# Twelve rewritten round orders, one rounding moved to ScalarE and one subtraction moved to VectorE in a fused attention and ReGLU kernel

## The chip, the cores and the metric

The kernel runs on one core of one Trainium2 chip. The metric is the device time in microseconds (us) of one execution of the whole program; lower is better. The core has five engines with a queue each: TensorE (PE) multiplies, VectorE (DVE) and ScalarE (ACT) work element by element and can read TensorE's results, GpSimd (POOL) works element by element on the on-chip memory alone and issues DMAs, and SyncE (SP) issues DMAs. Every queue is worked off strictly in the order written.

## The reference

```python
x = A_x                                              # 2048 x 448, float32
g = sigmoid((x * gate_w).sum(-1))
qkv = x @ wqkv                                       # 16 heads of 28
p = softmax(q @ k.T * 28 ** -0.5); a = (p @ v) @ wo  # per head, 2048 x 2048
gate, up = B_x @ W_gate, B_x @ W_up                  # F = 1792; B_x is not used: x stands for it
b = (relu(gate) * up) @ W_down
out = g * a + (1 - g) * b
```

In `reference` the second block is called with the same `x`, so both halves read one input.

## The kernel before, in words

**Precision.** Most products are computed from a rounded high part and the remaining low part of each operand. Making such a pair is always two instructions: `act_high` (or `dve_high`) writes the rounded copy, then `low` (VectorE) or `pool_low` (GpSimd) subtracts it from the source.

**Stages.** (1) Up to 140 us: projections of q, k, v and the gate, written to DRAM, with the first 100 row-maximum matmuls and the first scores mixed in. (2) From 140 to 1051 us: 32 attention rounds, two per head, which also compute 54 of the 56 gate/up tiles. (3) The tail, from 1051 us on: the last two gate/up tiles, the down projection (`down`) and the output projection (`wout`).

**A round.** A round handles 8 of the 16 key tiles of a head. Its work is written by hand in a string, and `ROUNDS` says which string each round uses. Every letter emits one step, and the order of the letters is the order in which every engine's queue is filled:

- `s` + bank: a 128x512 score matmul; ScalarE takes it out with an exponential (`scores`, L265 and L267).
- `m` + bank: a row-maximum matmul for the next head; VectorE reduces it (`smax`, L242 and L243).
- `r` + bank: a score matmul whose softmax shift is not known yet; ScalarE copies it out raw (`raw_scores`, L273 and L277). `d` is VectorE's running maximum over it (`raw_max`, L281), and the bank is free only after both.
- `e`: ScalarE's exponential of a raw tile (`raw_exp`, L304), after GpSimd subtracted the shift from it (`raw_less`, L300).
- `x`: one of the 10 full-height matmuls of a gate or an up half (`gu_mm`, L612). Ten accumulate in one bank. A round with 40 of them holds banks 4, 5, 6 and 7 in turn; a round with 20 holds 4 and 5.
- `u`, `U`, `l` (first round only): the splitting of gate/up weight tiles 0 and 1 (`split_f`) and a delayed store of the projections.

There are eight PSUM banks. The digit behind a letter is its bank; in the listings below, the banks 0 to 7 are called `b_69` to `b_76`. Banks 0 to 3 are always open to `s`, `m` and `r`; 6 and 7 only until the round's second tile needs them. A matmul into a bank waits until the engine that reads the bank's last result is done.

Behind the string, a round issues the last, half-height matmul of each gate/up half (two at a time, in the two halves of the array), then `relu` and `hidden`, the splitting of the next round's weight tiles, the exponentials that are left (`while len(exps) > ROUNDS[r + 1].count("e")`: all but those that the next string names), and 64 matmuls that multiply probabilities with V (`pv`, L650), in groups of four side by side. Nothing else for TensorE is issued during `pv`, so the two evicting engines catch up there.

Strings by name: FIRST and SECOND (rounds 0 and 1), AA (rounds 2, 4, 6, 10, 12, 14, 18, 20, 22), BA (3, 7, 11, 15, 19, 23), BB (5, 13, 21), DA (8, 16), BC (9, 17), CA (24, 26), CB (25, 27), AY, BY, AZ, BZ (28 to 31).

**The tail.** `fetch_o` loads a 512-token block of the attention output into the tile `or`, of which there is one buffer; `split_o` makes its high and low parts (`on`) in two pieces; `wout` multiplies them. `split_d` prepares the next hidden tile (`hh`) and, for the first 14, a tile of W_down (`WD`): ScalarE rounds, VectorE subtracts. `fetch_d` loads their sources over the SP queue, two tiles ahead of the `split_d` that uses them. `fetch_o` for the second block stands on the same SP queue, ahead of the loads for the thirteenth hidden tile.

Of the kernel before, what the change touches and what calls it, by code (L numbers as in the profile page):

```python
# [45 lines left out]

FIRST = ("m2m3m6m7s0s1uxxxxs0xm2lxxxxUs3xxs6s1m7xm0xs2m3xs1m7xxm2xxr0r1r3xm7s2dxr0dxxr7ds2xr1dxr3xs2dxr0dxxxdm"
         "2s1xm3xxm0s1xm2xm3xm1s0xxm2xm3s0xm1xs2m0m2m1m0")  # L50

SECOND = ("xs0r1m2s6xm7dxs3xs0m2r6xs7m3dxs1xm0xs2m7xs3r1m6xs0xds2xm7xs3m6r0s1xxdm2s7xm3s1xr0s7xm2dxs1m3xs7xm2s1"
          "xs0r7m3xs1xdm2s0xm3s1xxm0r2xs1s3dxm0xxs1m2s3xm0xs1r2m3xs0xds1xm3xs0m2s1xxxm0s2")

AA = ("xm0s1xr2m6s7xm3xs1xm2s0xr7m6xs1dxm3s0xm2xr6s1xm7dxs0m3xs2m1xr7exm0s2dxm3s1exxm0s2xr7em1s3xdm2xes0xm1"
      "xs3xexm2r0s1m3xdexs2xm1s3xexm0r2m1s3xdexm0xxs3em1s2xxm0s3xm1s2xm0xxr1s2m0d")
# [4 lines left out]
BA = ("xs0m1r2s7xm6ds3xs0m1r7xs6m3ds0xr2s1m6xds3xm0s7xr1s6m3s2dxm7s0xr6s3m2xds1m0xs7r3xs2m1s6dxm7s0r2xs1m6x"
      "ds3m0xs7r1s6xm2xds7m0xs6")

AY = ("xs0m1s2xr6m7s3m0xs2r6xm1s3s7dxm2r0s1xm3ds7xm6s2r1s3xm7xds0m2s6r3xes7m0xds1m6xem2s0xr7s3s1xm6des0m2xs"
      "3xm6es1xm7em0xs2r3s6xm1r7xds2s0m1m6d")

BY = ("xs0r1ds2xs6xr7ds3xs0xs2r6ds1exs3xs0r7dexs2s1xxr6des3xs0xs7xr2des1xs6xs3xs0xr7ds2s1s6xxr0dxs2s7s1")

AZ = ("xs0xs1xxs2xxs6xs7xxs3xs0xxs1xxs2xs7xxs3xs0xxs1xxs2xs3xxs0xxs1xs2exxs3xs0exxs1xxs2exs0xxs1xx")

BZ = ("xs0xs1xxs2xxs6xs7xxs3xs0xxs1xxs2exs7xxs3xes0xxs1xxes2xs3xxs0exxs1xs2xexs3xs0xxs1xxs2xs0xxs1xx")

DA = ("xs0m1xs2r6m7xxm3s0xm2xs1r6m7xs0xdm3xs2r1m7xs0m6dxxs3m2xs7xm0r3xs1m2dxm7s0xr1xs2xdm0m3xs7m2xs1xem0r7x"
      "s3m1exds2xm0s3r1xexm2xdm3s0exxm2xxs0em1s3xxm2s0exm1r3xs2em0xds1xxm2s0xm1")

BC = ("xm0s1r2xm7s6xdxm3s1xem0xs7r6m2exs1xdm3xs0em7xr2xs6m1xds3m0xxm7s1xr3xm2s0dxm1s7xm2xs0xm3r7xs1m0dxs2xm"
      "3xs1m0xr2xm3s1dxm0xxs3m1xs2xr0m3xs1dm2xxs3xm1s0xm2r3xs1m0dxs2xxs1m0")

CA = ("xm0s1xr2m6s7xm3xs1m2xs0xr7m6xs1dm3xm0s2xxr6m1s7xdm3xs2xm0s7xr1m2xs3dxm7s0xm2xs3r1m0exs7xdm2xs3em0xr1"
      "m7xs2em3xds0xxem2xm3s0m1xexs2xr0m3xes1dm2xxs3xem1s0xm2m3xes1m0xs2xxm1xr0s2m1d")  # L80

CB = ("xs0m1r2s7xm6ds3xm0s1r7xes6m3s2dxm1exr0s3m6xs7s2dxm1exr6m3xs7s0s2dm1xr3xs7m6s0xdm2s1xr7s6m0s3dr1xs2xm"
      "6s0dm3s7xm2s6r0xs7m1xds6xm2s7")
# [17 lines left out]
def gated_mix_kernel(ctx, tc, x, wq, wo, wgu, wd, out):  # L101
# [55 lines left out]
    def low(dst, src, high):  # L157
        nc.vector.tensor_tensor(dst, src, f32(high), op=OP.subtract)  # L158

    def pool_low(dst, src, high):  # L160
        nc.gpsimd.tensor_tensor(dst, src, f32(high), op=OP.subtract)  # L161
# [426 lines left out]
    def split_f(i, high, low, part=(0, 1)):  # L588

        if part[0] == 0:  # L590
            WS[i] = fe.tile([P, 2, 7, P], F32R, name=f"wg_{i}", tag="wg", bufs=2)
        w, wr = WS[i], WR[i]
        for s in part:
            high(w[:, s, 0:3], wr[:, s, 0:3])
            low(w[:, s, 3:6], wr[:, s, 0:3], w[:, s, 0:3])
        if part[-1] == 1:
            high(w[:, :, 6], wr[:, :, 3])
            for s in range(2):
                rows = lane(1 - (2 * i + s in SECOND))
                low(w[rows, s, 6], wr[rows, s, 3], w[rows, s, 6])  # L600
            del WR[i]
# [206 lines left out]
    ON, OR, GA, DR, HH, ACC = {}, {}, {}, {}, {}, {}  # L808
# [191 lines left out]
```

## Time and profile before

| what | value |
|---|---|
| median of 3 runs | 1241.53 us (1241.13 to 1241.87) |
| the profiled execution's own time | 1241.64 us |
| its span, first to last instruction | 1239.9 us |
| granted TensorE clock | 1.00 in every slice |
| busy: PE, PE weight loads | 1228.2 us, 858.5 us |
| busy: DVE, ACT, POOL | 896.9, 842.9, 627.5 us |
| matmuls with weight loads | 6447 |

The times and the profile come from one program without any other load on the chip. A row of the timeline gives the start, the length, the engine, the line, the operation, the tiles (written <- read), the count of instructions that were merged into the row, and in brackets the engine's idle time ahead of it with what ended it. Consecutive matmuls overlap in the records (a 128x512 matmul's record is 0.39 us long, but the next begins about 0.23 us after it), so a small brake on TensorE shows in the distance between starts and hardly in the busy share.

### The profile page before, as it was taken

Reading aid. Unit: us, or ns where it says so; the run is one execution under the profiler, and the core shown is the slowest. Engines: PE = TensorE matmul, PEld = TensorE weight load, DVE = VectorE, ACT = ScalarE, POOL = GpSimd, SP = SyncE. Lnnn points to the kernel's source line nnn. Section 1 sums busy time; section 2 is a strip of 40 time slices with the busy share of each in tenths; the row PEclk is TensorE's granted clock in tenths of the full one; section 3 lists DMA queues with packets and bytes.
Section 4 is the critical chain, followed back from the end, with each engine's and each line's share of the span. In section 5 each row is a group of like instructions: output and inputs, shape, how many; then the busy total and the mean of one; then the engine's idle time right before and its main releaser. Section 6 shows DMA issues by size and latency. Waiting matters only on the chain.

```text
span 1239.9 us, 18801 instructions
## 1 busy us (share of the span) xinstructions
PE 1228.2 (99%) x6447; PEld 858.5 (69%) x6447; DVE 896.9 (72%) x1442; ACT 842.9 (68%) x1673; POOL 627.5 (51%) x702
## 2 busy tenths in 40 slices
PE   9999999999999999999999999999999999999998
PEld 6888766666656665666666666666565655989997
DVE  6488879787878787797878787878787734563342
ACT  5312667988797877968787988797887895522121
POOL 4332325574738384838384665647482677431020
PEclk9999999999999999999999999999999999999999
DMA  8966514141434232333524141425231122853432
GB/s 308 344 240 245 179 52 153 54 129 60 137 95 145 75 122 82 107 97 107 166 96 135 57 129 60 137 80 159 75 110 43 48 85 91 273 172 110 140 107 80
DMA packets 62035, 157.64 MB, mean 127 GB/s; under 512 B 12994, under 2 KB 19746, under 8 KB 57514
## 3 DMA queue, kind: packets, MB, share of 16 engines
q1 hardware_dynamic: 47924, 111.47, 29.0%
q0 software_dynamic: 13584, 44.52, 9.9%
q8 instruction: 50, 0.82, 0.3%
q10 hardware_dynamic: 432, 0.46, 0.1%
q14 instruction: 45, 0.37, 0.1%
HBM read 108.70 MB, written 48.16 MB: 127 GB/s over the span
## 4 chain that ended last, share of the span: by engine, by line
PE 83%; ACT 7%; DMA 3%; POOL 3%; DVE 2%; issue 1%; SPq 0%; DVEq 0%; POOLq 0%; ACTq 0%
PE b L612 17%; PE b L650 16%; PE b L242 13%; PE b L265 12%; PE b L900 9%; PE b L436 6%; PE b L273 4%; ACT P L267 3%; PE b L454 3%; PE b L855 3%; ACT P L304 1%; POOL V L300 1%; ACT V L304 1%; ACT V L277 1%; DVE wg L155 1%
## 5 line engine op out<-in xcount | busy, mean ns | idle before, releaser
L243 DVE TENSOR_REDUCE mx<-b 128x1 f32<-128x512 f32 x784 | 519.2, 686 | 61.9 <-PE b L242 55.4
L267 ACT ACTIVATE P<-b 128x512 f32<-128x512 f32 x780 | 446.7, 610 | 130.1 <-PE b L265 115.3
L612 PE MATMUL b<-X,wg 128*128 128x512 f32 (+1 forms) x1232 | 429.5, 400 | 0.3 <-POOL wg L161 0.3
L242 PE MATMUL b<-K,Q 128*128 128x512 f32 x784 | 310.6, 399 | 2.8 <-DVE mx L243 1.4
L265 PE MATMUL b<-Q,K 128*128 128x512 f32 x784 | 309.9, 398 | 1.1 <-ACT P L267 0.8
L612 PEld LDWEIGHTS b<-X,wg 128*128 128x128 f32 (+1 forms) x1232 | 219.6, 188 | 62.2 <-issue 22.1
L650 PE MATMUL b<-P,v 128*32 128x512 f32 x1800 | 226.2, 594 | 0.0
L242 PEld LDWEIGHTS b<-K,Q 128*128 128x128 f32 x784 | 147.0, 188 | 52.5 <-ACT P L267 16.2
L265 PEld LDWEIGHTS b<-Q,K 128*128 128x128 f32 x784 | 146.9, 188 | 48.1 <-ACT P L267 16.4
L634 POOL DMA_DIRECT2D h_d<-rl x56 | 31.4, 561 | 291.0 <-DVE rl L628 248.5
L300 POOL TENSOR_TENSOR P<-P,V 128x512 f32<-128x512 f32 x120 | 150.9, 1293 | 26.6 <-DMA V<-mr_d 26.6
L650 PEld LDWEIGHTS b<-P,v 128*32 128x32 f32 x1800 | 61.7, 110 | 144.4 <-issue 144.2
L161 POOL TENSOR_TENSOR wg<-wgr,wg 128x384 fp32r<-128x384 f32 x216 | 155.0, 732 | 9.8 <-DVE wg L155 1.2
L300 POOL TENSOR_TENSOR V<-V 128x512 f32<-128x512 f32 x120 | 150.8, 1292 | 11.9 <-DMA V<-mr_d 11.9
L281 DVE TENSOR_TENSOR V<-b,V 128x512 f32<-128x512 f32 x215 | 145.9, 679 | 3.3 <-ACT P L277 1.6
L900 PE MATMUL b<-WD,hh 128*128 128x448 f32 x672 | 138.3, 366 | 2.2 <-DVE hh L158 1.4
L900 PEld LDWEIGHTS b<-WD,hh 128*128 128x128 f32 x672 | 126.1, 188 | 13.2 <-DVE hh L158 2.2
L152 ACT ACTIVATE hh<-hr 128x512 fp32r<-128x512 f32 x56 | 35.3, 631 | 110.5 <-PE b L900 106.8
L650 PE MATMUL b<-V,v 128*32 128x512 f32 x248 | 110.1, 593 | 0.0
L273 PE MATMUL b<-Q,K 128*128 128x512 f32 x240 | 96.2, 402 | 0.0
L158 DVE TENSOR_TENSOR hh<-hr,hh 128x512 fp32r<-128x512 f32 x56 | 46.8, 836 | 62.0 <-ACT hh L152 62.0
L277 ACT ACTIVATE V<-b 128x512 f32<-128x512 f32 x116 | 70.1, 609 | 9.6 <-PE b L273 8.7
(100 smaller groups left out, 1125.5 us busy)
## 6 DMA issues: line engine op xcount, KB each, us to landing
wgr<-wgu SPq DMA_DIRECT2D x55, 512.0 KB
K<-qk_d SPq DMA_DIRECT2D x64, 224.0 KB
Q<-qk_d SPq DMA_DIRECT2D x64, 224.0 KB
h_d<-rl POOLq DMA_DIRECT2D x56, 256.0 KB, 3.3
hr<-h_d SPq DMA_DIRECT2D x56, 256.0 KB
qk_d<-st POOLq DMA_DIRECT2D x21, 512.0 KB, 4.9
X<-x_d SPq DMA_DIRECT2D x24, 256.0 KB
x_d<-X POOLq DMA_DIRECT2D x5, 1024.0 KB, 5.6
```

The source lines that it names most:

```text
L161: nc.gpsimd.tensor_tensor(dst, src, f32(high), op=OP.subtract)
L242: nc.tensor.matmul(ps, Q[h][:, u * P:(u + 1) * P], K[h % 3][:, c * TB:(c + 1) * TB], start=True, stop=True)
L243: nc.vector.tensor_reduce(MX[h][:, 4 * u + c:4 * u + c + 1], ps, axis=AX.X, op=OP.max)
L265: nc.tensor.matmul(ps, K[h % 3][:, kt * P:(kt + 1) * P], Q[h][:, j * TB:(j + 1) * TB], start=True, stop=True)
L267: nc.scalar.activation(prob(i, j), ps, AF.Exp, scale=SCALE)
L273: nc.tensor.matmul(ps, K[h % 3][:, kt * P:(kt + 1) * P], Q[h][:, 3 * TB:], start=True, stop=True)
L277: nc.scalar.activation(own, ps, AF.Copy)
L281: nc.vector.tensor_tensor(run, ps, run if i % NK > 1 else prob(i - 1, 3), op=OP.max)
L300: nc.gpsimd.tensor_tensor(own, own, piece(TOP), op=OP.subtract)
L612: nc.tensor.matmul(ps, WS[i][rows, s, a], xf(i // NF, b)[rows], start=(n == 0), stop=(n == NT - 1))
L650: nc.tensor.matmul(po[32 * j:32 * j + 32], VH[h][:, i % NK], prob(i, j), start=(i == i0), stop=(i == i0 + ni - 1))
L900: nc.tensor.matmul(ACC[i // NF][t][:, :D], HH[i][:, a, t * P:(t + 1) * P], WD[:, f, b], start=(f == 0 and n == 0), stop=(f == NF - 1 and n ...
```

## The change

Twelve of the strings are new; BB gets one `d` moved behind one `x`, and BC is dropped, its two rounds now using BB. Each string still holds the same number of `x`, `s` and `r`. SECOND has 27 `m` instead of 25 and the two CA rounds 28 instead of 29, so their sum is the same. The `e` of CB (3), BC (3) and two of BY's four are gone from the strings, and DA has 8 instead of 7, so more exponentials are issued at the end of the round before (CA, DA) or of the same round (BY).

```diff
-FIRST = ("m2m3m6m7s0s1uxxxxs0xm2lxxxxUs3xxs6s1m7xm0xs2m3xs1m7xxm2xxr0r1r3xm7s2dxr0dxxr7ds2xr1dxr3xs2dxr0dxxxdm"
-         "2s1xm3xxm0s1xm2xm3xm1s0xxm2xm3s0xm1xs2m0m2m1m0")
+FIRST = ("m2m3m6m7s0s1uxxxxs0xm2lxxxs7xs0xUxm3xs1m7s6xm2s3m0m7xxxs2m1xm0s7m6r3m2r1xr7xxr3xxr2dr0dr1ddddxxs7xxx"
+         "s3s2xm7m0xxs1m3xxm2xm1s3m0xxm2xr3m1xxdxm0xm2s1")
...
-ROUNDS = [FIRST, SECOND, AA, BA, AA, BB, AA, BA] + [DA, BC, AA, BA, AA, BB, AA, BA] * 2
+ROUNDS = [FIRST, SECOND, AA, BA, AA, BB, AA, BA] + [DA, BB, AA, BA, AA, BB, AA, BA] * 2
...
             elif o == "U":
-                split_f(1, dve_high, pool_low)
+                split_f(1, act_high, pool_low)
...
         act_high(ON[tb][0][:, c], OR[tb][:, c])
-        pool_low(ON[tb][1][:, c], OR[tb][:, c], ON[tb][0][:, c])
+        low(ON[tb][1][:, c], OR[tb][:, c], ON[tb][0][:, c])
```

(The new file is three lines shorter, so its line numbers are lower by three.)

**VectorE in the first round.** Here `wg` is a split weight tile, `wgr` the weights as loaded, `mx` the row maxima and `pair` the delayed store. Before:

```order
L158 TENSOR_TENSOR pair<-b_74,pair 128x512
L155 CAST wg_1235<-wgr_1195 128x384 x2
L155 CAST wg_1235<-wgr_1195 128x2x128
L243 TENSOR_REDUCE mx_931<-b_76 128x1
L243 TENSOR_REDUCE mx_931<-b_69 128x1
```

Now:

```order
L155 TENSOR_TENSOR pair<-b_74,pair 128x512
L240 TENSOR_REDUCE mx_931<-b_72 128x1
L240 TENSOR_REDUCE mx_931<-b_76 128x1
L240 TENSOR_REDUCE mx_931<-b_71 128x1
L240 TENSOR_REDUCE mx_931<-b_69 128x1
```

The three casts of weight tile 1 have left VectorE's queue; they stand on ScalarE's, behind five exponentials of the round and the copy of `pair`.

**TensorE in the middle of a round AA** (round 4; matmuls 61 to 69 of its 99 ahead of the half-height ones, counted from 0). Before:

```order
L242 MATMUL b_71<-K_128,Q_131 128x512
L273 MATMUL b_69<-Q_130,K_127 128x512
L265 MATMUL b_70<-Q_132,K_129 128x512
L242 MATMUL b_72<-K_128,Q_131 128x512
L612 MATMUL b_75<-X_121,wg_2162 128x512
L612 MATMUL b_75<-X_120,wg_2162 128x512
L265 MATMUL b_71<-Q_132,K_129 128x512
L612 MATMUL b_75<-X_120,wg_2162 128x512
L242 MATMUL b_70<-K_128,Q_131 128x512
```

Now, matmuls 61 to 70:

```order
L262 MATMUL b_70<-Q_132,K_129 128x512
L262 MATMUL b_76<-Q_132,K_129 128x512
L239 MATMUL b_72<-K_128,Q_131 128x512
L609 MATMUL b_75<-X_120,wg_2166 128x512
L262 MATMUL b_71<-Q_132,K_129 128x512
L239 MATMUL b_69<-K_128,Q_131 128x512
L262 MATMUL b_70<-Q_132,K_129 128x512
L609 MATMUL b_75<-X_121,wg_2166 128x512
L262 MATMUL b_72<-Q_132,K_129 128x512
L239 MATMUL b_76<-K_128,Q_131 128x512
```

Bank 7 (`b_76`) still takes scores and maxima here, where the old string had only banks 0 to 3 left for them.

**ScalarE at the border of a CA and a CB round** (rounds 24 and 25; `P` are raw score tiles, `mr` the copied maxima that open round 25). Before:

```order
L152 ACTIVATE wg_8090<-wgr_7936 128x2x128
L304 ACTIVATE P_1043<-P_1043 128x512
L304 ACTIVATE P_1085<-P_1085 128x512
L304 ACTIVATE P_1129<-P_1129 128x512
L304 ACTIVATE P_1163<-P_1163 128x512
L304 ACTIVATE P_1208<-P_1208 128x512
L261 ACTIVATE mr_8143<-b_75 12x128
```

Now:

```order
L149 ACTIVATE wg_8090<-wgr_7936 128x2x128
L301 ACTIVATE P_1043<-P_1043 128x512
L301 ACTIVATE P_1085<-P_1085 128x512
L301 ACTIVATE P_1129<-P_1129 128x512
L301 ACTIVATE P_1163<-P_1163 128x512
L301 ACTIVATE P_1208<-P_1208 128x512
L301 ACTIVATE P_1238<-P_1238 128x512
L301 ACTIVATE P_1276<-P_1276 128x512
L301 ACTIVATE P_1327<-P_1327 128x512
L258 ACTIVATE mr_8146<-b_75 12x128
```

All eight exponentials of the second half now stand ahead of `mr`, during `pv`; three of them stood between the scores of round 25.

More of the change, by code (lines that the diff above doesn't have):

```diff
@@ L43 @@
 AHEAD = 100
-FIRST = ("m2m3m6m7s0s1uxxxxs0xm2lxxxxUs3xxs6s1m7xm0xs2m3xs1m7xxm2xxr0r1r3xm7s2dxr0dxxr7ds2xr1dxr3xs2dxr0dxxxdm"
-         "2s1xm3xxm0s1xm2xm3xm1s0xxm2xm3s0xm1xs2m0m2m1m0")
[L52 to L56, printed above, removed]
@@ L58 @@
-BB = ("xs0r1m2xs7m6dxm3xs0xr2s7xm6dxs1m0xm3xs7xm6r1s2xm0dxs7xm3xr2s0m7xds1xm3xm0s7xr1m2xs3dm7xs0xr2m3xs1dxm"
-      "0xxs3m1xs2xxm0r3s1m2xdxs0xxm1s2xm0s3xm1s2xm0r3xm1s2dxs0xxm1m2xs0")
[L61 to L83, printed above, removed]
-ROUNDS = [FIRST, SECOND, AA, BA, AA, BB, AA, BA] + [DA, BC, AA, BA, AA, BB, AA, BA] * 2
+FIRST = ("m2m3m6m7s0s1uxxxxs0xm2lxxxs7xs0xUxm3xs1m7s6xm2s3m0m7xxxs2m1xm0s7m6r3m2r1xr7xxr3xxr2dr0dr1ddddxxs7xxx"
+         "s3s2xm7m0xxs1m3xxm2xm1s3m0xxm2xr3m1xxdxm0xm2s1")
@@ new lines @@
+SECOND = ("xs1m2s0xm6s7m1xs2m3xr6m7ds1m0r2xs3dxs7xs6xm3xm0s1xm2s6m3xs7m0s2r6m1dxs3r7xm0xdr1xs3m6dxs0xs2xs3m6s0m"
+          "7xm1s2xm3xs0xm2s7m1xs0xxm3xm1m0s2r7s3xxr1xs2xddr0m3xxxs2xs1xs3dxxm0xs1m2xs3s0xm1s2")
+AA = ("xs2m7m0s1m6r3xm2s7xm1s3xm0r6xm2r3dxs1s7s0xxxxdxm2es7s3m6s1xm0r2r7m3dxdxxs6xs0xm1m3ees2xxm6xs1s7m0m3x"
+      "m2xeexxs1s7m3xs2m0s1xs3m7r2m0xxm3xr1xeddxxexm3xs2em0xr1xs3xs2edxm0xxm3s1m2")
+DA = ("xs7m6s1xxs3m0s2m7s1xm6m3s2xr7s0xm6xr2m7dr3s1s6m0xxdr7xm1s2s0xxm6xm2s3s1xs0xdm6s3exm2xm7s6r1m3r0xxdxm"
+      "2s7xxxdm1exem2xs0m7xexs1m3s0xxxem1r2m0xxxs3dxxem1s0xm3s2xeem1xxm3m0r2dxs1")
@@ new lines @@
+BB = ("xs0r1m2xs7m6xdm3xs0xr2s7xm6dxs1m0xm3xs7xm6r1s2xm0dxs7xm3xr2s0m7xds1xm3xm0s7xr1m2xs3dm7xs0xr2m3xs1dxm"
+      "0xxs3m1xs2xxm0r3s1m2xdxs0xxm1s2xm0s3xm1s2xm0r3xm1s2dxs0xxm1m2xs0")
+BA = ("xs0xs1m2s3xm6m7r0xds3r1m6xs2xs7xdr3m0ds6xm2s1xs7m0r6xs3s1s7dxxm2r3s0m1xs6m7dr2xxs0m1s6xs7dxs0s1m6s3m"
+      "7m2r0xs6xr1s7dm3dxs2m6s0")
+CA = ("xs0m2r6xm7s3xm1s0m6s2xm3xxm1r0m2s7s3xr6dm1dxxs2m0xs7m3xs1s2xs6m7xr3m1xxxdr6m2s1dxxes7xm3m1xs0exem7xx"
+      "m2s1m3s0xs7xm1s2m3xxm7m0er1s2xxds7m3xer0m2xdxs1m3exxs2xxm1exs0m3xr2xs1em0xd")
@@ new lines @@
+CB = ("xs2m7r0xs3m6dr1s7dxxm3m6s2r7s0xs1m3dxs2xs0m6s3m1s2s7m0s6xm3xr1xs0dxr2m3s7dxs6s1m0xm7s3m2s6r1xdxs0s3r"
+      "6xm7m2s0dxxs1xm7r0s3m2xs6d")
+AY = ("r6s7m2s1m0s6r7m3xr0ds2s6xdm3s1xs2m7s0m6xs3s1m7xs2m3r6r1xxs7dxdes2m0exxm7s6m1xs2xm3r0em7dxxs6s1xm3xem"
+      "7s6m0xs1s3m2m7s6r0m1xxm3der2s7s6ds1x")
+BY = ("xs7r2ds0s1xxxr3s7xs0s6dxr1s7ds2xr0s6s3xs7xs1xs2xdr6xds7s0xr3s2edxxxer0xxs1s2xs6xs3ds7r1s2ds0s6")
+AZ = ("xxs0xs1xxs2xs6xs3xxxs0xs7xxs3xs2xs6xs3xs2xs0xxxxs3s2xxs0xs1xxs7xexxs3xs0xxes1xxs2xxs0exs1xx")
@@ L86 @@
+BZ = ("xs6xs0s7s1xxxxs0xs3s1xxs0xxxs3s1xxxes6s3s7s0xs2xxxxs1xxxs0s3xs7xxs1xxexxxexexs2s0s3xxxxs2exxx")
+ROUNDS = [FIRST, SECOND, AA, BA, AA, BB, AA, BA] + [DA, BB, AA, BA, AA, BB, AA, BA] * 2
 ROUNDS += [CA, CB, CA, CB, AY, BY, AZ, BZ]
```

## The prediction

> **What bounds the kernel now.** I read the page first, then the chain of waits, then the timelines of the places that the chain names.
>
> ```profile
> PE 1228.2 (99%) x6447; PEld 858.5 (69%) x6447; DVE 896.9 (72%) x1442; ACT 842.9 (68%) x1673; POOL 627.5 (51%) x702
> ```
>
> TensorE is the bound, but its 99% hides brakes, since records overlap. The chain of waits shows them better: it has the start of each round's `pv` block, so the difference of two rows is one round.
>
> ```profile
> 165.64 7.00 PE b L650 x64
> 197.50 7.00 PE b L650 x64
> 229.06 7.01 PE b L650 x64
> 252.75 7.00 PE b L650 x64
> 284.14 7.00 PE b L650 x64
> 314.39 7.00 PE b L650 x64
> 345.78 7.00 PE b L650 x64
> 369.46 7.00 PE b L650 x64
> 400.87 7.00 PE b L650 x64
> ...
> 837.02 7.00 PE b L650 x64
> 868.99 7.00 PE b L650 x64
> ...
> 926.05 7.00 PE b L650 x64
> 951.16 7.00 PE b L650 x64
> 976.93 7.00 PE b L650 x64
> 997.72 7.01 PE b L650 x64
> ```
>
> SECOND takes 197.50 - 165.64 = 31.86 us for 105 matmuls ahead of the half-height ones, BB (round 5) 314.39 - 284.14 = 30.25 for 98. Seven matmuls more cost 1.61, or 0.23 each, which is the distance of two matmuls that nothing holds up. So these two strings have next to no brakes, and BB is a yardstick: 30.25 plus or minus 0.23 per matmul. Against it:
>
> - AA (round 4, 99 matmuls): 31.39, yardstick 30.48, 0.9 too long; nine such rounds.
> - DA (round 8, 99): 31.41, 0.9 too long; two.
> - CA (round 24, 101): 31.97, yardstick 30.94, 1.0 too long; two.
> - BA (round 3, 68 matmuls, one tile): 23.69. CB (round 27, 69) is 25.11, 1.2 above BA plus one matmul; AY (round 28, 72) is 25.77, again 1.2 above BA's measure; BY (round 29, 52) is 20.79, 0.8 above it.
> - FIRST (88): from its first matmul at 140.51 (below) to 172.64 it takes 32.13; yardstick 27.95; 4.2 too long.
>
> With AA 9 x 0.9, DA 1.8, CA 2.0, CB 2.4, AY 1.2, BY 0.8 and FIRST 4.2, some 20 us stand above the yardsticks; that is the ceiling for these strings.
>
> Who holds TensorE up? The evicting engines. Their pace when never idle:
>
> ```profile
> 158.97 7.35 DVE L243 TENSOR_REDUCE mx<-b 128x1 f32<-128x512 f32 x12
> ```
> ```profile
> 995.58 3.12 ACT L267 ACTIVATE P<-b 128x512 f32<-128x512 f32 x6
> ```
> ```profile
> 287.18 3.74 ACT L304 ACTIVATE V<-V 128x512 f32<-128x512 f32 x7
> ```
>
> 7.35 / 12 = 0.61 per maximum, 3.12 / 6 = 0.52 per exponential with the last one's tail (0.49 without, (3.12 - 0.60) / 5 being 0.50), 3.74 / 7 = 0.53 per raw exponential. I use 0.61, 0.49 and 0.53.
>
> **The change part by part.**
>
> *FIRST and the moved rounding.* TensorE's first matmul of the round, its two stops, and what VectorE did in the first of them:
>
> ```profile
> 140.51 1.20 PE L242 MATMUL b<-K,Q 128*128 128x512 f32 x4 [0.33 <-DVE mx L243]
> ```
> ```profile
> 147.92 0.39 PE L265 MATMUL b<-Q,K 128*128 128x512 f32 x1
> 149.33 0.50 PE L242 MATMUL b<-K,Q 128*128 128x512 f32 x1 [1.02 <-DVE mx L243]
> ```
> ```profile
> 145.42 3.25 DVE L155 CAST wg<-wgr 128x384 fp32r<-128x384 f32 x3
> ```
> ```profile
> 163.89 1.09 PE L242 MATMUL b<-K,Q 128*128 128x512 f32 x3 [0.42 <-ACT P L267]
> ```
>
> The three casts keep VectorE from the maxima for 3.25 us; the gap of 1.41 between 147.92 and 149.33 is 1.18 beyond a matmul's 0.23. In the new string the casts are ScalarE's, where such a tile costs half of this row of two tiles, 1.19 us:
>
> ```profile
> 166.41 2.37 ACT L152 ACTIVATE wg<-wgr 128x384 fp32r<-128x384 f32 x6
> ```
>
> ScalarE has 16 `s` and 8 `r` here, 24 x 0.49 = 11.8 us, in over 25 us, so 1.19 has cover; without it a score's bank would come free up to 1.19 late. GpSimd's subtractions follow the rounding wherever it runs; the string needs tile 1 at its 21st `x`, now at matmul 48 rather than 44, some 11 us into the round. The reload (`fetch_f(3)`) and the V load behind it on SP move a microsecond at most, and nothing in this round needs them. The second named brake is the old string's end, `s2m0m2m1m0`: banks return after 2, 3 and 5 matmuls (0.46 to 1.15 us), less than a VectorE or ScalarE turn; the new shortest distance is 6. I take 1.2 + 0.6 for these two and half of the other 2.4: 3.0 us. Ends: 1.2 (the cast alone) and 4.2.
>
> *AA, DA, CA.* One brake of AA:
>
> ```profile
> 275.57 0.39 PE L612 MATMUL b<-X,wg 128*128 128x512 f32 x1
> 276.04 0.50 PE L242 MATMUL b<-K,Q 128*128 128x512 f32 x1
> ```
>
> The gap is 0.47 instead of 0.23. It is the last matmul of the old AA piece shown above: its bank 1 was filled six matmuls earlier, and 6 x 0.23 = 1.4 us must hold the end of the score matmul and a ScalarE queue with other work in it. From matmul 49 on, the old AA has only banks 0 to 3 for `s`, `m` and `r`. The new AA uses bank 6 until matmul 50 (old: 25) and bank 7 until 70 (old: 48), just ahead of the 21st and 31st `x` that need them (56 and 79). The mean distance at which a bank comes back, counted in the strings, grows from 8.0 to 9.1 matmuls; DA 8.2 to 8.9, CA 8.0 to 8.8. The engines' load does not change: VectorE 34 x 0.61 = 20.7 us of AA's 99 x 0.23 = 22.8, ScalarE 32 x 0.49 + 9 x 0.53 = 20.5. BB has the same 34 VectorE evictions in 98 matmuls and no brakes, so the load permits it. Bounds per round: a loss, if the bunches in the new strings (up to five `x` in a row) starve an engine, and 0.9. I take 0.5 for AA and 0.45 for DA, nearer the yardstick, since part of the 0.9 is a start and an end that the strings share: 9 x 0.5 + 2 x 0.45 = 5.4. CA 0.4 x 2 = 0.8; its matmul fewer per round is paid back by SECOND's two more. The first `e` of AA moves from matmul 37 to 29, 6.7 us into the round; GpSimd has its first tile ready before that (round 4 starts at 259.7, the first of these four ends at 265.2):
>
> ```profile
> 263.88 5.04 POOL L300 TENSOR_TENSOR P<-P,V 128x512 f32<-128x512 f32 x4 [2.11 <-DMA V<-mr_d]
> ```
>
> *CB.* ScalarE was given 32 x 0.49 + 3 x 0.53 = 17.3 us in 69 x 0.23 = 15.9 us: an overrun of 1.4, close to the 1.2 by which CB exceeds BA. Without the three `e` it is 15.7, as in BA. They go in front of `mr`, where ScalarE idled:
>
> ```profile
> 876.24 0.27 ACT L261 ACTIVATE mr<-b 12x128 f32<-12x128 f32 x1 [2.64 <-PE b L251]
> ```
>
> 3 x 0.53 = 1.6 fits in 2.64; without that idle time the next round's first exponentials would wait. Gain 2 x 1.1 = 2.2; bounds 0 and 2.4.
>
> *BA, AY, BY, AZ, BZ, BB in BC's place, SECOND.* BA: 0.2 x 6 = 1.2, from 0 to 0.5 each. AY and BY stay overloaded on ScalarE (BY: 32 x 0.49 = 15.7 us in 12.0, whatever its `e`): 0.3 + 0.2. BZ has this:
>
> ```profile
> 1041.38 0.50 PE L265 MATMUL b<-Q,K 128*128 128x512 f32 x1 [0.56 <-ACT P L267]
> ```
>
> Four of its five `e` move from matmuls 29 to 47 to between 48 and 61, behind the scores they delayed: 0.8. BC to BB: 0.2 each, 0.4. SECOND, AZ and the one moved `d` of BB: 0, since they have nothing to lose their cover against but the same queues.
>
> *The tail.* TensorE stops twice:
>
> ```profile
> 1089.48 2.30 PE L900 MATMUL b<-WD,hh 128*128 128x448 f32 x10 [1.40 <-DVE hh L158]
> ```
> ```profile
> 1097.01 3.03 PE L900 MATMUL b<-WD,hh 128*128 128x448 f32 x12 [0.77 <-ACT hh L152]
> ```
> ```profile
> 1083.76 5.12 POOL L161 TENSOR_TENSOR on<-or,on 128x1024 fp32r<-128x1024 f32 x2 [8.29 <-ACT on L152]
> ```
> ```profile
> 1086.57 2.86 DVE L158 TENSOR_TENSOR hh<-hr,hh 128x512 fp32r<-128x512 f32 x1
> ```
> ```profile
> 1088.91 0.38 SPq L832 DMA_DIRECT2D or<-o_d x1
> ```
>
> While GpSimd makes the low parts of `on`, VectorE's subtraction takes 2.86 instead of 0.69 and ends at 1089.43, which is when TensorE starts again. On VectorE a piece costs about 1.22, by this row:
>
> ```profile
> L158 DVE TENSOR_TENSOR X<-xr,X 128x1024 fp32r<-128x1024 f32 x3 | 3.7, 1222 | 2.2 <-ACT X L152 2.2
> ```
>
> Queue by queue: `on` 1083.7 to 1084.9, `WD` 0.6, `hh` 0.7, so `hh` is ready at about 1086.2, before it was needed (1089.48 - 1.40 = 1088.1): the first stop goes, 1.4 to 1.6. Behind the waiting subtraction stand only `WD` and `hh` of later tiles. The second stop stays: its hidden tile was loaded behind `fetch_o` on SP, which waits until `or` is free; that is now 1087.3 instead of 1088.9, 1.6 earlier, just as much as TensorE arrives earlier. The other six pieces are 7.3 us of VectorE work in a stretch where it is busy 54 of 140 us:
>
> ```profile
> 1100.00:1240.00 140.00, 135.82 (x671) 125.59 (x669) 54.00 (x73) 30.68 (x46) 20.25 (x18) 1.00 0.37 115
> ```
>
> Without that cover each would add 1.22. I take 1.6; bounds 0 and 2.5 (both stops).
>
> The stretched row agrees with the Trainium skill, SBUF — State Buffer, section "Who interferes with whom": a VectorE instruction with two on-chip inputs and a GpSimd instruction that reads on-chip memory exclude each other for a whole instruction. By that rule the new subtraction, which also has two such inputs, would shut GpSimd out in turn, 1.22 at a time; in the tail GpSimd then has only DMA issues left, so the sum by the rule is the same.
>
> **Sum.** 3.0 + 5.4 + 0.8 + 2.2 + 1.2 + 0.5 + 0.8 + 0.4 + 1.6 = 15.9 us off the profiled 1241.64, whose span is 1239.9; the median of the runs, 1241.53, is 0.1 lower. 1241.5 - 15.9 = 1225.6.
>
> **The rivals.**
>
> - *Only the edits with a named cause pay.* The cast and the end of FIRST (1.8), CB (2.2), BZ (0.8), the tail (1.6): 6.4, so 1235.1. For it: AA's brakes are 0.1 to 0.25 each and can come back elsewhere in a new string. Against: the banks stay open longer there.
> - *Nearly all brakes go.* The 20 us of the list, BA, BZ, BC and the tail at their full size, 20.5 + 3 + 0.8 + 0.5 + 2.5 = 27 at most; some start and end loss stays in every round, so about 1217.
> - *Slower: the bunches starve an engine.* Runs of `x` in AA and DA (five and three, against two) leave VectorE without input; it has 22.8 - 20.7 = 2.1 us to spare in a round. If more than that is lost in the 11 rounds, TensorE pays. The other terms give 10.5, so it decides against the change once AA and DA are each over 1.0 longer than before; at 1.5 longer it gives 1241.5 - 10.5 + 16.5 = 1247.5. Against: five `x` are 1.2 us, and a queue two maxima deep covers that.
> - *No effect*: gains and such losses cancel, about 1241.
>
> **How the numbers follow.** Chances: the sum (gains of 10 to 20) 0.52, named causes only 0.22, nearly all 0.11, starving 0.11, no effect 0.04. Predicted is 1225.6. The range is 1217.5 to 1239.0: below it lies most of the "nearly all" case (0.07), above it, where the gain falls under 0.2% (2.5 us, about what a measurement of this kernel can tell from no change), the "starving" and "no effect" cases less the lightest starving (0.13); 0.2 in all. Faster (under 1239.0) 0.85, within 0.2% 0.05, slower 0.10.
>
> **What would show it.** No row of VectorE casts in FIRST, and that round near 29 us; AA near 30.9, DA 31.0, CB near 24.0 between `pv` starts; ScalarE's idle time ahead of `mr` down to about 1 us at round 25; in the tail no `hh` over 1 us around the first output block, one TensorE stop of about 0.8 left, and the second `or` load about 1.6 us earlier against the last `pv`. The prediction is wrong if AA rounds stay at 31.4 or exceed it, or if ScalarE's weight casts push scores back in FIRST.

## The result, and the profile after

The changed kernel takes 1228.29 us (median of five runs, 1226.41 to 1231.61) against 1241.53 before (also five, 1241.13 to 1241.87): ratio 0.9894, 95% interval 0.9877 to 0.9912, 13.2 us less. 15.9 were predicted (1225.6). The profiled execution was the longest of its five (1231.61, span 1229.8), 10.0 us below the profiled execution of before; so what is read from it below accounts for 10 us and not for the medians' 13.2.

The page's busy times and the starts of the `pv` blocks in the chain of waits, which give the rounds as before (line numbers are three lower now):

```profile
PE 1218.5 (99%) x6447; PEld 865.4 (70%) x6447; DVE 894.0 (73%) x1447; ACT 844.8 (69%) x1676; POOL 609.6 (50%) x694
```
```profile
227.06 7.00 PE b L647 x64
250.32 7.00 PE b L647 x64
281.09 7.00 PE b L647 x64
...
515.66 7.00 PE b L647 x64
545.87 7.00 PE b L647 x64
577.58 7.00 PE b L647 x64
...
832.37 7.01 PE b L647 x64
863.35 7.00 PE b L647 x64
887.37 7.00 PE b L647 x64
```

BA (round 3) takes 250.32 - 227.06 = 23.26, AA (4) 30.77, BB (13) 30.21, CA (24) 30.98 and CB (25) 24.02, but AA (14) takes 31.71. These distances over all rounds, from the profiles of before and after (for the table each from the end of one block to the end of the next; FIRST from the last projection matmul on, so that it is 0.7 longer than where the prediction counts from):

| rounds | before | after | sum | predicted |
|---|---|---|---|---|
| FIRST | 32.79 | 30.16 | -2.6 | -3.0 |
| SECOND | 31.86 | 32.28 | +0.4 | 0 |
| AA x9 | 31.37 to 31.57 | 30.76 to 34.33 | +2.1 | -4.5 |
| DA x2 | 31.42, 31.53 | 30.68, 30.74 | -1.5 | -0.9 |
| BC to BB x2 | 30.50 | 30.21 | -0.6 | -0.4 |
| BA x6 | 23.68 | 23.25 | -2.5 | -1.2 |
| CA x2 | 31.96 | 30.95 | -2.0 | -0.8 |
| CB x2 | 25.11 | 24.00 | -2.2 | -2.2 |
| AY and BY | 46.55 | 44.92 | -1.6 | -0.5 |
| AZ and BZ | 45.99 | 45.80 | -0.2 | -0.8 |
| tail, behind the last `pv` block | 189.23 | 189.92 | +0.7 | -1.6 |

Most strings give what was predicted or more, FIRST and AZ with BZ give less, and AA, SECOND and the tail lost. The named places: in FIRST VectorE takes seven maxima in a row where the casts stood, and ScalarE has the rounding; ahead of round 25's `mr` ScalarE idles 0.89 instead of 2.64. In order, from the timelines of VectorE and ScalarE:

```profile
146.44 4.49 DVE L240 TENSOR_REDUCE mx<-b 128x1 f32<-128x512 f32 x7 [0.82 <-PE b L239]
```
```profile
145.95 1.25 ACT L149 ACTIVATE wg<-wgr 128x384 fp32r<-128x384 f32 x3
870.60 0.27 ACT L258 ACTIVATE mr<-b 12x128 f32<-12x128 f32 x1 [0.89 <-PE b L248]
```

The long AA rounds have one stop each. TensorE and the SP queue in the longest (round 10, from 427.2 on), and TensorE's waits on loads over the whole span:

```profile
441.89 0.39 PE L609 MATMUL b<-X,wg 128*128 128x512 f32 x1
444.11 0.47 PE L239 MATMUL b<-K,Q 128*128 128x512 f32 x1 [1.83 <-DMA wgr<-wgu]
...
447.09 0.63 PE L609 MATMUL b<-X,wg 128*128 128x512 f32 x1
447.52 0.63 PE L262 MATMUL b<-Q,K 128*128 128x512 f32 x1
```
```profile
433.23 0.33 SPq L292 DMA_DIRECT2D mr_d<-V  x1
435.63 0.34 SPq L293 DMA_DIRECT2D V<-mr_d  x1
436.03 3.11 SPq L220 DMA_DIRECT2D Q<-qk_d  x4
439.25 0.35 SPq L223 DMA_DIRECT2D Q<-z_d  x1
```
```profile
PE b L239 <- DMA wgr<-wgu: 3.2, 3, 1.8
PE b L239 <- DMA Q<-qk_d: 0.5, 1, 0.5
```

The matmul at 444.11 is the first row maximum of a new head. Its Q was issued between 436.03 and 439.6, because SP first waits for the small store and load of the softmax shift (`mr_d`). The wait is put down to `wgr`, but this matmul reads only K and Q, so it is the same late Q. Such stops stand in rounds 6, 10, 14, 18 and 22: 1.06, 2.00, 0.89, 0.64 and 0.69 us beyond a matmul's distance, 5.3 in all. In rounds 4, 12 and 20, where the new head starts 20 matmuls later in the round, there is none, and these take 30.8, where 30.9 was predicted.

The tail, by the timelines of TensorE, VectorE and SP, and the last long row of the chain of waits, of before and of after:

```profile
1084.28 3.05 PE L897 MATMUL b<-WD,hh 128*128 128x448 f32 x12 [0.43 <-ACT hh L149]
```
```profile
1074.02 0.69 DVE L155 TENSOR_TENSOR hh<-hr,hh 128x512 fp32r<-128x512 f32 x1
```
```profile
1075.90 0.38 SPq L829 DMA_DIRECT2D or<-o_d  x1
```
```profile
1201.78 34.06 PE b L900 x168
```
```profile
1191.07 34.73 PE b L897 x168
```

One stop of 0.43 is left of 1.40 and 0.77, no `hh` around the first output block exceeds 0.7, and the second `or` load leaves 2.3 us earlier against the last `pv` matmul (1050.12 before, 1039.40 now). But the 168 matmuls of one block now take 34.73 instead of 34.06: 206.7 ns apart where it was 202.7, from this stop to the end. Over some 700 matmuls that is 2.8 us, more than the stops gave.

### The profile page after: what moved, and what is told of

Same layout as the page of the kernel before. It is cut to its first block, busy times and chain, and to the rows that moved or that the text cites. A ratio compares the mean times of both kernels' runs of the same rounds, so it can differ in the third digit from the quotient of the medians.

```text
span 1229.8 us, 18893 instructions
## 1 busy us (share of the span) xinstructions
PE 1218.5 (99%) x6447; PEld 865.4 (70%) x6447; DVE 894.0 (73%) x1447; ACT 844.8 (69%) x1676; POOL 609.6 (50%) x694
## 4 chain that ended last, share of the span: by engine, by line
PE 87%; DMA 5%; DVE 2%; ACT 2%; SPq 2%; issue 1%; POOL 0%; DVEq 0%; ACTq 0%; POOLq 0%
PE b L609 20%; PE b L647 15%; PE b L239 14%; PE b L262 13%; PE b L897 9%; PE b L433 6%; PE b L270 4%; PE b L451 3%; PE b L852 3%; ACT P L264 1%; DMA wgr<-wgu 1%; DMA K<-qk_d 1%; SPq L220 1%; DMA or<-o_d 1%; DVE V L289 1%
## 5 line engine op out<-in xcount | busy, mean ns | idle before, releaser
L240 DVE TENSOR_REDUCE mx<-b 128x1 f32<-128x512 f32 x784 | 509.4, 686 | 49.5 <-PE b L239 47.1
L264 ACT ACTIVATE P<-b 128x512 f32<-128x512 f32 x780 | 433.0, 619 | 115.8 <-PE b L262 108.6
L609 PE MATMUL b<-X,wg 128*128 128x512 f32 (+1 forms) x1232 | 411.4, 401 | 0.0
L239 PE MATMUL b<-K,Q 128*128 128x512 f32 x784 | 298.0, 393 | 4.9 <-DMA wgr<-wgu 3.2
L262 PE MATMUL b<-Q,K 128*128 128x512 f32 x784 | 291.6, 394 | 0.4 <-DVE os L653 0.2
L631 POOL DMA_DIRECT2D h_d<-rl x56 | 31.6, 564 | 287.3 <-DVE rl L625 282.8
L270 PE MATMUL b<-Q,K 128*128 128x512 f32 x240 | 92.8, 395 | 0.3 <-DVE os L653 0.3
L155 DVE TENSOR_TENSOR hh<-hr,hh 128x512 fp32r<-128x512 f32 x56 | 39.7, 709 | 59.1 <-ACT hh L149 59.1
L274 ACT ACTIVATE P<-b 128x512 f32<-128x512 f32 x116 | 70.3, 614 | 14.6 <-PE b L270 12.9
```

The source lines that it names most:

```text
L239: nc.tensor.matmul(ps, Q[h][:, u * P:(u + 1) * P], K[h % 3][:, c * TB:(c + 1) * TB], start=True, stop=True)
L240: nc.vector.tensor_reduce(MX[h][:, 4 * u + c:4 * u + c + 1], ps, axis=AX.X, op=OP.max)
L262: nc.tensor.matmul(ps, K[h % 3][:, kt * P:(kt + 1) * P], Q[h][:, j * TB:(j + 1) * TB], start=True, stop=True)
L264: nc.scalar.activation(prob(i, j), ps, AF.Exp, scale=SCALE)
L270: nc.tensor.matmul(ps, K[h % 3][:, kt * P:(kt + 1) * P], Q[h][:, 3 * TB:], start=True, stop=True)
L609: nc.tensor.matmul(ps, WS[i][rows, s, a], xf(i // NF, b)[rows], start=(n == 0), stop=(n == NT - 1))
```

## The experiments

**1. The late Q load, by its place in the queue** (changed kernel):

```diff
+            load_q(h + 3)      # ahead of raw_top, which has the mr_d store and load
...
-        if r % 2 and h + 3 < H:
-            load_q(h + 3)
```

> The changed kernel, with the load of Q for the head after next issued on the SP queue ahead of the two small DMAs of the softmax shift instead of behind them. Theory A (late Q): the waits of 0.6 to 2.0 us at the 35th matmul of rounds 6, 10, 14, 18 and 22 are gone, these rounds take 30.8 like rounds 4, 12 and 20, the matmuls at half rate behind the longest wait in round 10 are gone too, and the time falls by 2 to 6 us from the changed kernel's, to 1222 to 1226, with less spread between runs. Theory B (the order of AA): no change, 1226 to 1231.

Measured: 1264.87 us (1262.28 to 1271.39), ratio to before 1.0197 (1.0174 to 1.0219). The time rose instead of falling, and AA took 32.8 to 37.3. TensorE at the new head in round 10 of this kernel:

```profile
457.78 0.39 PE L609 MATMUL b<-X,wg 128*128 128x512 f32 x1
458.00 0.39 PE L239 MATMUL b<-K,Q 128*128 128x512 f32 x1
461.29 0.50 PE L270 MATMUL b<-Q,K 128*128 128x512 f32 x1 [2.67 <-ACT P L264]
```

The first maximum of the head no longer waits, here as in rounds 6, 14, 18 and 22: it starts 0.22 behind the matmul before it. So what it had waited for was Q. But TensorE now stops two matmuls later, at a raw score. Waits of round 4 in this kernel and its SP queue there:

```profile
POOL P L297 <- DMA V<-mr_d: 7.3, 1, 7.3
...
ACT P L301 <- POOL P L297: 4.3, 1, 4.3
PE b L270 <- ACT P L264: 3.7, 1, 3.7
```
```profile
256.95 3.06 SPq L220 DMA_DIRECT2D Q<-qk_d  x4
...
260.57 0.32 SPq L292 DMA_DIRECT2D mr_d<-V  x1
265.98 0.35 SPq L293 DMA_DIRECT2D V<-mr_d  x1
```

Behind the bulk of Q the small store takes 265.98 - 260.57 = 5.4 us from issue to the issue that waits for it, against 435.63 - 433.23 = 2.4 in round 10 of the changed kernel (1.6 in its round 4); over the span SP waits 51.0 us for the 15 small stores, against 21.0. The shift comes late, GpSimd and then the new AA's early `e` on ScalarE wait for it, and TensorE stands for 3.7. The order on SP is a trade, and the old one is the better. The run shows that the late Q made the stops and that AA hangs on SP's order, not yet that the new head's start is what pulled it into the Q load.

**2. The late Q load, by the head's start** (changed kernel with the old SECOND and CA: the maxima per string are the old ones again, so a new head starts at matmul 41 of an AA round instead of 34):

```diff
-SECOND = ("xs1m2s0xm6s7m1xs2m3xr6m7d…      (27 m)
+SECOND = ("xs0r1m2s6xm7dxs3xs0m2r6xs7m…    (25 m)
-CA = ("xs0m2r6xm7s3xm1s0m6s2xm3…           (28 m)
+CA = ("xm0s1xr2m6s7xm3xs1m2xs0xr7…         (29 m)
```

> The changed kernel with the old SECOND (25 maxima instead of 27) and the old CA (29 instead of 28), so that each new head's first maximum comes two maxima later in the round (matmul 41 instead of 34 after a two-tile round). Theory A (late Q): the waits in rounds 6, 10, 14, 18 and 22 shrink by the 1.6 us of seven matmuls, to 0 to 0.5; SECOND is 0.45 shorter; the two CA rounds are 0.8 to 1.0 longer each; in all 1 to 4 us faster than the changed kernel. Theory B: AA rounds unchanged, the time 1 to 2 us slower.

Measured: 1227.78 (1227.06 to 1228.47), ratio 0.9887 (0.9874 to 0.99). All stops at the new head are gone; AA is 30.8 to 31.1 (31.65 in round 2), round 10 30.99 instead of 34.33; SECOND 31.86, CA 31.97. The nine AA rounds now bring 3.5 us. The `pv` starts of rounds 9 and 10:

```profile
426.22 7.00 PE b L647 x64
457.21 7.00 PE b L647 x64
```

So the rounds answer as expected, but the time hardly does: it is 0.5 below the changed kernel's median, where 1 to 4 were expected. By the profiles AA and SECOND gain 6.0, of which the old CA gives back 2.1 and the tail 0.7, and the changed kernel's profile is 3.3 above its median.

**3. AA alone** (kernel before, with the new AA):

> The kernel before with the new string AA alone; the new head's first row maximum then comes at matmul 41 or later in rounds 6, 10, 14, 18, 22 (it has 25 maxima in SECOND as before). Theory A (the new AA is good everywhere, and the changed kernel's long AA rounds come from the Q load that arrives after the maximum which needs it): all nine AA rounds take 30.7 to 31.1 us, the time falls by 4 to 6, to 1235.5 to 1237.5. Theory B (the new AA itself starves an engine after a round with two tiles): rounds 6, 10, 14, 18, 22 take 31.5 or more here too, and the gain is 2 us or less.

Measured: 1239.27 (1237.51 to 1241.71), ratio 0.9981 (0.9973 to 0.999). AA 30.81 to 31.08, except 31.62 in round 2. So AA's own gain is 0.4 to 0.6 in eight of the nine rounds and nothing in round 2, 3.5 us in all in this profile, and is there without the other strings. The time fell by 2.3 us by the medians, less than the 4 to 6 expected; the profiled execution (1237.51) is the fastest of its ten. The `pv` starts of rounds 3 and 4 in the chain, 30.87 apart:

```profile
252.98 7.00 PE b L650 x64
283.85 7.00 PE b L650 x64
```

**4. What shortens AA: the longer use of banks 6 and 7, or the order?** Two pairs. First, banks handed out by the longest unused one: the old order with 6 and 7 used until matmuls 47 and 70; and experiment 2's kernel with them given up at 25 and 48, as in the old AA.

> The kernel before; in AA every step stays in its old place, but the banks are handed out anew, always the one unused longest, with bank 6 open until matmul 47 and bank 7 until 70 (old: 25 and 48). A bank then comes back after 8.8 matmuls in the mean instead of 8.0. Theory A (the longer use of banks 6 and 7 is what the new AA gains by): AA falls from 31.4 to 30.8 to 31.0. Theory B (the order of the steps is what counts): AA stays at 31.2 to 31.5.

> The changed kernel with the old SECOND and CA, and in the new AA every step in its new place but the banks handed out anew with bank 6 open only until matmul 25 and bank 7 until 48, as in the old AA (mean distance 8.0). Theory A (banks): AA rises from 30.8 to 31.1 back to 31.4 or more, nine rounds, about 4 us. Theory B (order): AA stays at 30.8 to 31.1.

Measured: 1254.6 (ratio 1.0101, 1.0084 to 1.0118) with AA at 32.6 to 33.0, and 1239.38 (0.9984, 0.9972 to 0.9997) with AA at 32.3 to 32.5 (33.05 in round 2). Both are longer than either hand-written string, so the hand-out itself hurt (probably since a bank with a raw score is free only after two engines, which this rule does not see). I repeated both with banks handed out by the earliest expected release.

> The kernel before, with AA's old order of steps, but its banks handed out anew (the one expected free earliest), 6 used until matmul 47 and 7 until 70 as in the new AA. If the longer use of banks 6 and 7 is what shortened AA: 30.8 to 31.0 against 31.4, about 5 us less in all, 1237. If the order of the steps is: 31.2 to 31.5, 1241.

> The changed kernel with the old SECOND and CA and AA's new order of steps, but with banks 6 and 7 given up where the old AA gave them up (matmuls 25 and 48), the banks handed out as in its companion. If the longer use of banks 6 and 7 is what shortened AA: 31.4 or more against 30.9, 1232 or more. If the order of the steps is: 30.8 to 31.1, 1228.

Measured: 1245.38 (1.0032, 1.0019 to 1.0045), AA 31.6 to 32.0; and 1234.13 (0.9938, 0.9923 to 0.9953), AA 31.6 to 31.9 (32.4 in round 2). `pv` starts of rounds 3 and 4 in the latter:

```profile
250.63 7.01 PE b L647 x64
282.25 7.00 PE b L647 x64
```

31.62: the new order without the longer use of the banks is no better than the old string's 31.40. But this rule also put the old order with the longer use above 31.4, so the hand-out itself still costs something, and how much is not known, since the new order with the longer use was not run by this rule. So neither pair separates the longer use from the order: what shortens AA by 0.4 to 0.6 is the new string as a whole, order and banks as written, and which of the two does it stays open. The mean distance at which a bank comes back, by which I had argued, is no measure: it was 8.8, then 8.7, in the old order with more banks (8.0 before), and AA got longer both times.

**5. CB alone** (kernel before without the three `e` in CB):

```diff
-CB = ("xs0m1r2s7xm6ds3xm0s1r7xes6m3s2dxm1exr0s3m6xs7s2dxm1exr6m3…
+CB = ("xs0m1r2s7xm6ds3xm0s1r7xs6m3s2dxm1xr0s3m6xs7s2dxm1xr6m3…
```

> The kernel before; from the old string CB only its three raw exponentials are struck, so they run at the end of the CA round ahead of it. Theory A (ScalarE was overloaded in CB by these three): CB falls from 25.1 to about 24.0, as far as with the new string, and CA stays at 32.0, in all 2.2 us less, 1239.3. Theory B (the new string's order of scores and maxima is what helped): CB stays above 24.7.

Measured: 1240.79, against 1242.81 for before on that chip (0.9986, 0.9975 to 0.9996). `pv` starts of rounds 24 and 25:

```profile
869.04 7.00 PE b L650 x64
893.05 7.01 PE b L650 x64
```

CB falls from 25.11 to 893.05 - 869.04 = 24.01, all of its gain in the changed kernel (24.16 in round 27); CA stays at 31.99 and 31.94. So the three `e` among CB's scores are what lengthened it; that it was by the sum of ScalarE's work, as the prediction counts it, fits but was not tried apart.

**6. The moved rounding alone** (kernel before):

```diff
             elif o == "U":
-                split_f(1, dve_high, pool_low)
+                split_f(1, act_high, pool_low)
```

> The kernel before; only the rounding of weight tile 1 in the first round is ScalarE's instead of VectorE's, in the old string. Theory A (VectorE's three casts made FIRST's long stop): the gap of 1.41 us ahead of the maximum is gone or under 0.5, and FIRST shortens by about 1.0 to 1.3, from 32.8 to 31.5 to 31.8. Theory B (the rounding costs as much on ScalarE, since it stands there ahead of scores and waits for the weights' DMA until 145.3): scores' banks come free later, and FIRST stays at 32.3 or more. The rest of FIRST's gain of 2.6 belongs to the new string.

Measured: 1241.32, against 1242.81 for before on that chip (0.9991, 0.998 to 1.0002), not to be told from no change by its time. FIRST is 31.93 instead of 32.79, between what was expected in the two cases, so 0.86 of its 2.63 us come from the moved rounding by itself and the other 1.8 from the new string. TensorE's largest gap there, and the chain of waits that leads to it:

```profile
147.90 0.39 PE L612 MATMUL b<-X,wg 128*128 128x512 f32 x1
148.41 0.50 PE L265 MATMUL b<-Q,K 128*128 128x512 f32 x1
```
```profile
145.65 1.25 ACT wg L152 x3
146.90 1.47 ACT P L267 x3
```

The gap is 0.51 instead of 1.41, so 0.28 beyond a matmul's 0.23 instead of 1.18. It is not a rest of the old stop: it stands ahead of a score (L265), one matmul earlier than the maximum (L242) that had waited for VectorE and now does not. The score waits for its bank, which ScalarE empties late, since the rounding now stands ahead of its exponentials. So the casts were the cause of the old stop, and in the old string a quarter of it comes back as a wait for ScalarE. In the changed kernel's FIRST no matmul around the rounding (145.95 to 147.20) is held up in this way.

**7. The tail alone** (kernel before):

```diff
         act_high(ON[tb][0][:, c], OR[tb][:, c])
-        pool_low(ON[tb][1][:, c], OR[tb][:, c], ON[tb][0][:, c])
+        low(ON[tb][1][:, c], OR[tb][:, c], ON[tb][0][:, c])
```

> The kernel before with one edit: VectorE instead of GpSimd subtracts the low parts of the attention output. Theory A (the stop ahead of the hidden tile was the lock-out of VectorE): the stop of 1.4 us is gone, the second of about 0.8 stays, the part behind the last pv block falls from 189.2 to about 187.6, the time to about 1239.9. Theory B (what a tail gains it gives back, because the down-projection matmuls after the remaining stop follow each other at 207 ns instead of 203, as they did in the changed kernel's profile): the stop goes as well, but the part behind the last pv block stays at 189 to 190 and the time at 1241 to 1242.

Measured: 1241.59 against 1241.57 (1.0002, 0.999 to 1.0014). VectorE at the first output block in before and with this edit, then TensorE's one remaining stop with it and its SP row:

```profile
1084.18 2.47 DVE L158 TENSOR_TENSOR WD<-wdr,WD 128x448 fp32r<-128x448 f32 x1 [0.72 <-ACT WD L152]
```
```profile
1086.11 0.62 DVE L158 TENSOR_TENSOR WD<-wdr,WD 128x448 fp32r<-128x448 f32 x1
```
```profile
1096.78 3.02 PE L900 MATMUL b<-WD,hh 128*128 128x448 f32 x12 [1.72 <-ACT hh L152]
```
```profile
1088.53 0.38 SPq L832 DMA_DIRECT2D or<-o_d  x1
```

The first stop is gone, and the second has grown from 0.77 to 1.72. Against the last `pv` matmul (at 1050.12 before and 1050.62 here) TensorE arrives at the second stop 1.7 us earlier, but `fetch_o`, behind which its hidden tile stands on SP, leaves only 0.9 earlier: the first block had landed later, ScalarE's first `on` from it being at 1083.87, 33.25 behind that `pv`, where before it was at 1082.64, 32.52 behind. The 0.7 of that is a transfer's and not the edit's; without it the load would have left 1.6 earlier, as forecast, and a stop near the old 0.77 would be left (not shown by a run). The whole change bears this out: there the first `on` is at 1071.24, 31.84 behind that `pv` and 0.7 earlier than before, and the load left 2.3 earlier, again 1.6 apart from the landing. The part behind the last `pv` block is 188.5, where 187.6 was expected in one case and 189 to 190 in the other; in the six kernels here that leave the tail as it was it is 188.5 to 192.0, so this one value tells little. The stretched row (2.47 before, 0.62 without GpSimd's subtraction beside it) agrees with the exclusion that the prediction quoted from the Trainium skill, SBUF — State Buffer, "Who interferes with whom": without the subtraction on GpSimd the stretch is gone.

**8. The changed kernel once more, and a version made from the findings.** Both on one chip beside the kernel before. The second is the changed kernel with the old SECOND and AZ, and with the 29th `m` put back into the new CA at a gap:

```diff
-…s6m7xr3m1xxxdr6m2s1dxxes7xm3…
+…s6m7xr3m1xm0xxdr6m2s1dxxes7xm3…
```

> The changed kernel once more, unedited, beside the others on one chip: 1226 to 1230 us. Late Q load: the AA rounds behind a two-tile round (6, 10, 14, 18, 22) again exceed those behind it (4, 12, 20) by 0.5 to 3 us in the profile, and by how much differs from the first profile, since a transfer's landing varies. If it was an accident of that one execution, all nine are 30.8 to 31.1. Distance of the down projection's matmuls behind the second stop: 206.7 ns again if it belongs to the program, 202.7 if to the execution.

> The changed kernel with the old SECOND and the old AZ, and the new CA with one maximum more (29, set into a gap near its middle), so that each new head's first maximum in an AA round comes at matmul 41 again. If the late Q load is what lengthened AA, and the two maxima more are what lengthened SECOND: AA 30.8 to 31.1, SECOND 31.9, CA 31.2 (30.9 and one matmul), AZ 22.5; against the changed kernel 0.75 x 9 + 0.4 + 0.7 less 0.5 = 7 us less in a profile with its stalls. By the medians, where the version with the old SECOND and CA gained 0.5 us only, 1225 to 1227. If AA is longer for the new strings' own sake, AA stays at 31.4 to 31.9 and the time at 1228.

Measured: 1229.92 (0.9906, 0.9891 to 0.9921) for the changed kernel. Its rounds 6, 10, 14, 18 and 22 have the stops again (0.85, 2.84, 0.70, 0.75 and, hardly one, 0.09), so they belong to the program; and the down projection is at 206.7 ns again. Round 10's stop, in the timeline:

```profile
445.04 0.47 PE L239 MATMUL b<-K,Q 128*128 128x512 f32 x1 [2.68 <-DMA wgr<-wgu]
```

The version takes 1225.56 (1224.17 to 1226.75), ratio 0.9869 (0.9853 to 0.9886), 4.4 below the changed kernel beside it. The `pv` starts of rounds 9 and 10:

```profile
426.04 7.00 PE b L648 x64
457.02 7.00 PE b L648 x64
```

AA in round 10 is 30.98; CA with its matmul more is 31.33 and 31.39, 0.1 to 0.2 above what was expected. The old AZ gives 22.52 instead of 23.28, but BZ behind it is 23.22 instead of 22.47 to 22.52: the two rounds together are 45.74 against 45.80, and hardly depend on the string.

## Why the prediction was right or wrong

The likeliest case (gains of 10 to 20 us) came, and the time lies in the range. The sum is 2.7 us too large by the medians (5.9 by the profile), made of errors of both signs, and that they nearly cancel is luck: the largest term, AA, came out as a loss of 2.1 instead of a gain of 4.5, and the sign that the prediction names for being wrong, AA rounds at 31.4 or above, is there in six of the nine rounds. DA, BA, CA, AY and BY made up for most of it.

- *CB* is right in size (2.2) and in its cause, the three `e` (experiment 5).
- *FIRST* is right within 0.4; of the parts, the rounding by itself brought 0.86 and not 1.2, since in the old string a score then waits for ScalarE (experiment 6). The scores that the prediction feared to see pushed back are not held up in the new string.
- *AA and SECOND: a step failed.* AA's 0.5 per round is nearly right for the string: 0.4 to 0.6 in eight rounds and nothing in round 2, 3.5 us in all and not 4.5 (experiments 2 and 3). What failed is "its matmul fewer per round is paid back by SECOND's two more", with 0 for SECOND. I counted the maxima as 0.23 us each and not as a place in a sequence: two more in SECOND bring every later head's first maximum seven matmuls (1.6 us) forward in AA, in front of its Q's landing. That costs 5.3 us in stops in the first profile and 5.2 in the second, of which some 0.2 a round come back, since later brakes of the same round fall away. Round 10 of the first profile pays about 1.6 us more for slow matmuls (last section), so AA stands at +2.1 instead of the string's own -3.5. The Q load's landing against that matmul was the margin to look up.
- *The longer use of banks*, the reason given for AA's gain, is neither shown nor refuted; the mean distance behind that argument is not its measure (experiment 4).
- *DA, BA, CA, AY and BY* gave 7.6 where 3.4 was taken (BA 0.42 a round, not 0.2; CA 1.0, of which 0.23 is the matmul fewer; AY and BY 1.6). I had held AY and BY to a ScalarE bound of 0.49 us per score. BY came to 19.88, 0.9 less than before, so that bound did not hold it; whether the two `e` fewer did it, and which part of the other strings gave the rest, was not tried.
- *AZ and BZ*: "0" and 0.8 are wrong singly (+0.7 and -0.9), as what one frees the other takes.
- *The tail: mis-sized.* The step "1.6 earlier, just as much as TensorE arrives earlier" holds only apart from the landing of the first block, which moved by 0.7 one way in experiment 7 and the other way in the whole change. By its time the edit alone cannot be told from no change (1.0002, an interval from 1.2 us less to 1.7 more). What the sum left out is the matmuls' distance of 206.7 or 202.7 ns, worth 2.8 us (last section). Among profiles with one and the same distance the part behind the last `pv` block is shorter with the edit: 187.6 to 188.5 against 188.5 to 189.5 at 202.7 ns, and 189.7 to 190.7 against 191.9 and 192.0 at 206.7. So the edit seems worth 1 to 2 us there, and the tail's +0.7 comes with the longer distance; these are single profiles, and some of them differ in other strings too.

Of the rivals, starving by bunches of `x` did not come: AA with its five `x` in a row is shorter than before wherever Q is there, round 2 apart. A slower AA did come, by another mechanism.

## What to carry to other kernels

A step that is moved by a count (two row maxima more in one round) moves everything that is numbered behind it. So look up, for each later stage, what its first user waits for, the loads above all, and how many microseconds lie between landing and use. Before a load is put ahead of another, see what small transfer on a critical path then stands behind its bytes. A stop that is taken away at one end of a chain is worth only what its next supplier can follow.

## What was not expected of the hardware

**A clock drop after a stop of 1.8 us, by chance.** In round 10 of the first profile of after, matmuls behind the stop start 0.43 us apart instead of 0.23 (the rows at 447.09 and 447.52 above). The busy time by stretches (length; busy time of PE, PEld, DVE, ACT and POOL; granted clock, DMA share, GB/s), in the first and then in the second profile of the changed kernel:

```profile
444.90:448.20 3.30, 3.30 (x9) 2.59 (x8) 2.39 (x4) 1.63 (x3) 3.30 (x4) 0.50 0.28 88
```
```profile
445.40:449.00 3.60, 3.60 (x17) 2.95 (x16) 3.34 (x6) 2.86 (x6) 3.60 (x4) 1.00 0.21 59
```

The granted clock was 0.50 for 3.3 us behind a stop of 1.83, and 1.00 behind one of 2.68 at the same place in the other execution. The Trainium skill, TensorE: Matmul & The Clock Gate, "What's actually happening", says that a free-running window of 3.4 us decides, and that the clock falls after at least one idle window. That the outcome changes between runs fits the free-running window; that a stop must be as long as a window does not, as 1.83 us were enough once.

The clock records of the traces say more. In the profile of experiment 1 the granted clock was 0.50 from 213.97 to 217.38, 271.99 to 278.82, 340.26 to 343.67, 756.68 to 760.10 and 821.54 to 824.95: stretches of 3.41 us or twice that, whose starts lie whole multiples of 3.413 us apart. In every other profile, too, the changes of the clock lie on such a grid. If one adds up TensorE's time without a matmul in each window of the grids, over all fourteen profiles and as far as the clock was full, every window with 1.96 us or more was followed by half rate, none with 1.75 or less, and three of the five between. The stop of 1.83 lay in one window (441.35 to 444.76); the one of 2.68 was cut by a border at 444.15 into 1.79 and 0.89. So here it took a window that was a little over half idle, and the chance is where the border falls.

**A spacing that stays.** The down projection's distance of 202.7 or 206.7 ns holds from the second stop to the end. It is 202.7 in before, in experiments 3, 5 and 7, in experiment 4's first pair and in the new order of its second. It is 206.7 in both profiles of after, in experiments 1 and 2 and in the version of experiment 8, but also in experiment 6 and in the old order of that second pair, whose instructions there are those of before. So it is no matter of the instructions behind the stop; 2.8 us hang on it. What sets it stays open.

Round 10's Q lands the latest of the five since its load is issued 1.8 us behind the end of the `pv` block ahead of it, where the other four have 0.7 to 0.9. SP waits there for the small store: from its issue to the issue behind it are 2.40 us in round 10 (433.23 to 435.63) and 1.33 to 1.48 in rounds 6, 14, 18 and 22. It is so in the second profile too (2.42 against 1.33 to 1.49), and in before (2.20). Why the store is slower in this round stays open.
